# One scan for the first block's chain, and a hand-written order of VectorE and ScalarE for the opening, in a linear-recurrence-and-experts kernel on one core

## Chip, cores, metric

One core of a Trainium2 chip runs the kernel. The metric is the device time of one execution in microseconds; the kernel before took 1793.38 (median of three runs, 1790.74 to 1793.52). TensorE (PE), VectorE (DVE), ScalarE (ACT), GpSimd (POOL) and the queues that issue DMAs (SP's above all) each work through a list of their own in order, and wait for each other by semaphores.

## What is computed

For 4 batches of 768 positions and 8 heads of 48 channels a complex recurrence runs over time, and its result feeds a mixture of 8 experts with Sinkhorn-balanced weights. Cut to what matters:

```python
scale = np.minimum(mag, 0.999) / (mag + 1e-06)      # mag = |a|
for t in range(S):
    S_re, S_im = a * S (complex) + k_t v_t^T         # kv goes into the real part
    y[t] = q_t @ S_re
x = y as [3072, 384]
P = softmax-like, 8 Sinkhorn passes over x @ w_gate
for e in range(8):
    out += P[:, e:e+1] * (np.maximum(x @ w1[e], 0) @ w2[e])
```

Precision is near fp32: a matrix operand is split into a high part and a residue (both fp32r), and each product is three matmuls (`hh*wh`, `hh*wl`, `hl*wh`).

## The kernel before

The 3072 rows are 12 *blocks* of 256 positions, and each block is two *chunks* of 128. Phase 1 goes over the blocks. Per block it has two kinds of work.

The **chain** (`elem`, `chain`, `scan`) normalises the decay `a` and multiplies it up along time within each chunk. `chain` begins with a square on ACT (L390), a sum on DVE (L391), two ACT steps (L392, L393), two DVE steps (L394, L395), an ACT step (L396), two DVE steps (L397, L398) and the product with `z` (L400). Then `scan` calls `cmul` twelve times: each call multiplies complex numbers with two products (L283, or L286 in pieces), a difference (L287) and a sum (L288), all on DVE. A closing part squares the result (ACT, L409), sums (DVE, L410), takes a root and a square (ACT, L413, L414), has three DVE steps (L415 to L417) and makes the decayed keys `kh` (L420) and queries `z` (L422), two halves each. For blocks 1 to 11 the chain runs at once over both chunks (128 x 768 elements per plane); for block 0 `elem` runs it twice, once per chunk, at 128 x 384.

The **mix** copies `kh` and `z` with 24 small DMAs into the per-head layout `ks` and `qs` (L441; six for each of `ks` and `qs` of each chunk, all on SP's queue). Then come, per chunk: transposed keys `ktp` (PE, L460, copied to `kt` by ACT, L462), `scores` (`sp`, PE L474, with a causal mask copied by DVE into `sc`, L477), the state increment `U` (PE, L469), small copies of the chunk's total decay (ACT, L502 to L504), the outputs `y` (PE, L491), the state update (DVE, L517 and L524 to L528, `st`), and the split of `y` into `xh` (ACT, L530) and `xl` (DVE, L531).

The **experts** 0 and 1 follow one block behind: 16 *expert steps* per block, each a layer-1 product `ph` (PE, L179 to L181, reading `xh` and `xl`), relu copies `hh` and `hf` (ACT, L185, L186) and the residue `hl` (DVE, L187); layer 2 (`po`, L158 to L160) runs three steps later. While block i is mixed, PE works on the expert steps of block i-1, and the mix's PE parts are put between them from step `LEAD[i]` on (11 for block 1). Phase 2 does the other six experts with a fast-matrix-multiplication scheme (L798 to L800, L894 to L896).

Ahead of the first expert step is the **opening**. Beside block 0's chain and mix it prepares the sixteen weights of experts 0 and 1. `load_w` handles twelve: DMA into a raw tile `wr` (L123; four raw tiles in turn), a rounded copy on ACT (L124), and for each half j a PE difference `wd` of raw and rounded (L128 by the identity, L129 by its negative) that ACT copies as residue (L130). The last four come as twelve pieces of 256 columns through `load_thirds` (L139, L140, L143 to L145), eight pieces ahead.

In phase 1 the order of PE is the order of the code (`manual_schedule` for PE alone). DVE, ACT and the DMA queues are ordered by the framework's scheduler, with hints: `issue_after` (emit behind another instruction), and `behind`, an ordering edge that puts a mask copy behind a `cmul` of the next block's scan.

Of the kernel before, what the change touches and what calls it, by code (L numbers as in the profile page):

```python
# [1 line left out]

# [12 lines left out]
C = H * D  # L15
# [39 lines left out]
class Net:  # L55
# [9 lines left out]
    def build(self):  # L65
# [3 lines left out]
        with ExitStack() as ctx:  # L69
# [30 lines left out]
            self.fl = cst.tile([128, ns * (NCT * NCH + 2) + 2], F32, name="fl")  # L100
# [18 lines left out]
    def load_w(self, e, f, wx):  # L119
# [3 lines left out]
        self.wl = nc.sync.dma_start(raw, self.w[e, f])  # L123
        nc.scalar.activation(t[:, 0, :], raw, AF.Copy)  # L124
        for j in range(2):
            cs = slice(j * C, j * C + C)
            d = (self.psB if j else self.psA).tile([128, C], F32, tag="po" if j else "ph", name=f"wd{e}_{f}_{j}")
            nc.tensor.matmul(d, self.ident, raw[:, cs], start=True, stop=False)  # L128
            nc.tensor.matmul(d, self.nident, t[:, 0, cs], start=False, stop=True)  # L129
            nc.scalar.activation(t[:, 1, cs], d, AF.Copy)  # L130

    def load_thirds(self, e, f, wx):
        nc = self.nc
        t = self.wt[e, f] = wx.tile([128, 2, 2 * C], F32R, tag="w", name=f"w{e}_{f}")
        for j in range(2 * C // SUB):
            cs = slice(j * SUB, j * SUB + SUB)
            raw = self.hp.tile([128, SUB], F32, tag=("hh", "hl")[(f * 3 + j) % 2], name=f"wr{e}_{f}_{j}")
            with self.tc.issue_after(self.wl.ins):
                nc.sync.dma_start(raw, self.w[e, f, :, cs])  # L139
            nc.scalar.activation(t[:, 0, cs], raw, AF.Copy)  # L140
            yield
# [3 lines left out]
            nc.scalar.activation(t[:, 1, cs], d, AF.Copy)  # L145

# [43 lines left out]
    def phase1(self, c1, ca):  # L190
# [29 lines left out]
        self.xs, self.vt, self.kqd, self.ql, self.masks, self.acts = {}, {}, {}, {}, {}, []  # L220
# [11 lines left out]
        for i in range(ns):  # L232
            mix = self.mix(i)
            if i == 0:
                n = 0
                while True:
                    with tc.issue_after(self.act0.ins), tc.issue_after(self.dve0.ins):
                        if next(mix, self) is self:
                            break
                    with tc.issue_after(self.act0.ins):  # L240
                        for _ in range(2):
                            if late and next(late[0], self) is self:
                                late.pop(0)
                                next(late[0], None) if late else None
                    n += 1
                for g in late:
                    for _ in g:
                        pass
# [5 lines left out]
            lg = self.logits(i - 1)  # L254
            for n in range(2 * NF):
# [7 lines left out]
            if i + 1 < ns:  # L263
                self.elem(i + 1)
# [3 lines left out]
        for f in range(2):  # L268
            self.moe.send((ns - 1, 0, f))
            next(lg)  # L270

    def cmul(self, L, R, n, alloc):
# [6 lines left out]

        a, b = tmp("a"), tmp("b")  # L280
        for o, k in ((a, 0), (b, 1)):
            if len(sh) == 4:
                V.tensor_tensor(o, L, R[:, k:k + 1].broadcast_to(sh), ALU.mult)  # L283
            else:
                for j in range(2):
                    V.tensor_tensor(o[:, j], L[:, j], R[:, k], ALU.mult)  # L286
        V.tensor_tensor(R[:, 0], a[:, 0], b[:, 1], ALU.subtract)  # L287
        self.last = V.tensor_tensor(R[:, 1], a[:, 1], b[:, 0], ALU.add)  # L288
        self.cm.append(self.last)
# [5 lines left out]
    def elem(self, i, scratch=False):  # L295
# [8 lines left out]
        if not scratch:  # L304
            with ExitStack() as st:
                if i > 1:
                    st.enter_context(self.tc.issue_after(self.ql[i - 2].ins))
                nc.sync.dma_start(z, self.aqk[i, :, 0:2])
            with self.tc.issue_after(self.ql[i - 1].ins):
                nc.sync.dma_start(qk, self.aqk[i, :, 2:4])  # L310
            nc.sync.dma_start(vt, self.v[i])

            def alloc(nm):
# [8 lines left out]
            self.chain(i, slice(0, NCH), zt, qk, alloc)  # L322
            return

        def cut(t, n):
            return t.rearrange("p a (c n) t -> p a c n t", n=NCH)[:, :, :, n, :]

        for n in range(NCH):
            for a in range(2):
                (nc.sync if a else nc.scalar).dma_start(cut(z, n)[:, a], cut(self.aqk[i, :, 0:2], n)[:, a])  # L330
        nc.sync.dma_start(qk, self.aqk[i, :, 2:4])
        nc.sync.dma_start(vt, self.v[i])
        kh = tmp.tile([128, 2, G, CH], F32, tag="kh", name="kh0", bufs=1)
        self.kqd[i] = (kh, zt)
        tt = {nm: self.xp.tile([128, G, CH], F32R, tag=tg, name=f"{nm}0").bitcast(F32)
              for nm, tg in (("x", "xh"), ("y0", "xl"), ("zz", "xh"), ("a", "xl"))}
        tt["b"] = tmp.tile([128, G, CH], F32, tag="t1", name="b0", bufs=5)
        tt["g0"] = tt["zz"]

        for n in range(NCH):  # L340
            def alloc(nm, n=n):
# [805 lines left out]
```

## Time and profile before

| | us |
|---|---|
| median of three runs | 1793.38 |
| lowest, highest | 1790.74, 1793.52 |
| the profiled execution | 1792.06 |
| its span (first to last instruction) | 1790.3 |
| PE busy | 1751.3 |
| DVE busy | 1366.8 |
| ACT busy | 733.6 |

The page shows one execution. Busy times are sums over instructions; neighbours on an engine overlap by about 0.1 us, so busy time can exceed the time from start to start. In rows of the timeline the columns are start, length, engine, line, operation, output and inputs, shape and count, and in brackets the idle time ahead of the first instruction and what ended it. In the view of waits each row has the total, how many times, and the longest. In rows of the view of windows, the window, its length, and busy time with instruction counts for PE, PEld, DVE, ACT and POOL, then the granted clock of PE, the mean share of the DMA engines, and GB/s. In the groups by line, the numbers behind the first bar are the busy time and the mean of one in ns.

### The profile page before, as it was taken

What the parts mean: (1) busy time and instruction counts of PE and PEld (TensorE: products, weight loads), DVE (VectorE), ACT (ScalarE), POOL (GpSimd) and SP (SyncE); (2) the same over time, 40 slices, a digit from 0 to 9 for tenths busy, and PEclk for the clock granted to TensorE, in tenths of its full rate; (3) what the DMA queues carried; (4) which work ended last, traced back from release to release, by engine and by line L of the source; (5) the groups of instructions that cost most, each with busy time, mean ns of one, the idle gap of its engine ahead of it and who ended that gap; (6) DMA issues with size and microseconds to landing.
All of it is one profiled execution on the core that took longest, in us unless ns stands there. A gap on an engine that the chain in (4) does not pass through costs nothing.

```text
span 1790.3 us, 30678 instructions
## 1 busy us (share of the span) xinstructions
PE 1751.3 (98%) x12024; PEld 1725.8 (96%) x12024; DVE 1366.8 (76%) x3036; ACT 733.6 (41%) x1609; POOL 6.4 (0%) x15
## 2 busy tenths in 40 slices
PE   5889999999999999999999999999999999999998
PEld 3889999999999999999999999999999999999998
DVE  7898999999983678777777767687767777776754
ACT  7544544555543544443332424243433333332321
POOL 1000000000000000000000000000000000000000
PEclk9899999999999999999999999999999999999999
DMA  6333333334343420111111101232111111010100
GB/s 215 95 119 110 119 119 119 119 114 119 103 105 104 135 89 27 53 53 46 45 54 50 48 18 54 76 111 63 45 52 38 54 54 50 22 54 18 45 27 29
DMA packets 133689, 132.85 MB, mean 74 GB/s; under 512 B 10400, under 2 KB 125856, under 8 KB 133536
## 3 DMA queue, kind: packets, MB, share of 16 engines
q1 hardware_dynamic: 132736, 130.41, 24.3%
q8 instruction: 96, 1.57, 0.4%
q14 instruction: 57, 0.47, 0.1%
q10 hardware_dynamic: 800, 0.39, 0.1%
HBM read 88.22 MB, written 23.59 MB: 62 GB/s over the span
## 4 chain that ended last, share of the span: by engine, by line
PE 91%; DVE 6%; DMA 1%; ACT 1%; issue 1%; SPq 0%; ACTq 0%; DVEq 0%
PE po L800 11%; PE po L799 11%; PE po L798 11%; PE P L894 10%; PE P L896 10%; PE P L895 10%; PE po L158 4%; PE ph L180 4%; PE ph L181 4%; PE ph L179 3%; PE po L159 3%; PE po L160 3%; PE sp L474 2%; PE y L491 2%; PE U L469 1%; DMA wr<-in_w_dram 1%
## 5 line engine op out<-in xcount | busy, mean ns | idle before, releaser
L800 PE MATMUL po<-wc,hl 128*128 128x384 f32 x1152 | 385.0, 334 | 0.0
L799 PE MATMUL po<-wc,hh 128*128 128x384 f32 x1152 | 384.8, 334 | 0.0
L798 PE MATMUL po<-wc,hh 128*128 128x384 f32 x1152 | 384.8, 334 | 0.0
L914 ACT ACTIVATE hh<-c 128x384 fp32r<-128x384 f32 x384 | 201.6, 526 | 347.0 <-DVE c L904 347.0
L919 DVE SCALAR_TENSOR_TENSOR hl<-c,hh 128x384 fp32r<-128x384 f32 x384 | 212.5, 553 | 50.5 <-ACT hh L914 36.3
L909 ACT ACTIVATE s<-P 128x384 f32<-128x384 f32 x192 | 94.1, 490 | 317.8 <-PE P L896 317.8
L800 PEld LDWEIGHTS po<-wc,hl 128*128 128x128 f32 x1152 | 216.3, 188 | 0.3 <-DVE hl L919 0.2
L798 PEld LDWEIGHTS po<-wc,hh 128*128 128x128 f32 x1152 | 216.3, 188 | 0.0
L799 PEld LDWEIGHTS po<-wc,hh 128*128 128x128 f32 x1152 | 216.3, 188 | 0.0
L185 ACT ACTIVATE hh<-ph 128x256 fp32r<-128x256 f32 x192 | 73.5, 383 | 231.1 <-PE ph L181 230.6
L180 PE MATMUL ph<-xl,w 128*128 128x256 f32 x576 | 162.7, 282 | 3.3 <-DVE xl L531 3.3
L181 PE MATMUL ph<-xh,w 128*128 128x256 f32 x576 | 162.4, 282 | 0.0
L179 PE MATMUL ph<-xh,w 128*128 128x256 f32 x576 | 162.0, 281 | 0.0
L894 PE MATMUL P<-B,wa 128*128 128x384 f32 x480 | 160.8, 335 | 0.1
L896 PE MATMUL P<-B,wa 128*128 128x384 f32 x480 | 160.3, 334 | 0.0
L895 PE MATMUL P<-B,wa 128*128 128x384 f32 x480 | 160.3, 334 | 0.0
L158 PE MATMUL po<-w,hh 128*128 128x384 f32 x384 | 136.7, 356 | 0.0
L159 PE MATMUL po<-w,hh 128*128 128x384 f32 x384 | 129.6, 337 | 0.0
L160 PE MATMUL po<-w,hl 128*128 128x384 f32 x384 | 129.4, 337 | 0.0
L904 DVE TENSOR_TENSOR c<-P,u 128x384 f32<-128x384 f32 x192 | 106.7, 556 | 22.0 <-PE P L896 20.4
L187 DVE TENSOR_TENSOR hl<-hf,hh 128x256 fp32r<-128x256 f32 x192 | 81.0, 423 | 48.3 <-ACT hf L186 46.9
L180 PEld LDWEIGHTS ph<-xl,w 128*128 128x128 f32 x576 | 108.8, 189 | 4.0 <-DVE xl L531 4.0
(189 smaller groups left out, 3579.0 us busy)
## 6 DMA issues: line engine op xcount, KB each, us to landing
raw<-in_w_dram SPq DMA_DIRECT2D x96, 384.0 KB, 3.1
qs<-z SPq DMA_DIRECT2D x144, 64.5 KB, 2.6
qk<-in_aqk_dram SPq DMA_DIRECT2D x12, 768.0 KB, 4.7
ks<-kh SPq DMA_DIRECT2D x144, 64.0 KB, 2.6
ye_d<-yst SPq DMA_DIRECT2D x48, 192.0 KB, 1.9
y<-ye_d SPq DMA_DIRECT2D x48, 192.0 KB, 2.4
z<-in_aqk_dram SPq DMA_DIRECT2D x11, 768.0 KB, 6.6
B<-x_d SPq DMA_DIRECT2D x40, 192.0 KB, 3.4
```

What stands on the lines that cost most here:

```text
L158: nc.tensor.matmul(po[k], hh[:, s], w2h, start=f == 0, stop=False)
L179: nc.tensor.matmul(ph, w[:, 0, cs], xh[:, ct, :], start=(ct == 0), stop=False)
L180: nc.tensor.matmul(ph, w[:, 0, cs], xl[:, ct, :], start=False, stop=False)
L181: nc.tensor.matmul(ph, w[:, 1, cs], xh[:, ct, :], start=False, stop=(ct == NCT - 1))
L798: nc.tensor.matmul(po[k], hh[:, s], w2[:, 0, i], start=first, stop=False)
L799: nc.tensor.matmul(po[k], hh[:, s], w2[:, 1, i], start=False, stop=False)
L800: nc.tensor.matmul(po[k], hl[:, s], w2[:, 0, i], start=False, stop=last)
L894: nc.tensor.matmul(ps, t[:, 0, k], x[:, 0], start=first, stop=False)
L895: nc.tensor.matmul(ps, t[:, 0, k], x[:, 1], start=False, stop=False)
L896: nc.tensor.matmul(ps, t[:, 1, k], x[:, 0], start=False, stop=last)
L914: A.activation(hh, c, AF.Relu)
L919: V.scalar_tensor_tensor(hl, c, 0.0, hh.bitcast(F32), ALU.max, ALU.subtract)
```

## The change

1. Block 0's chain runs once over both chunks, as for the other blocks. Its planes come in two DMAs of 128 x 768 elements instead of four of half the size. The two products of L400 become one instruction for all blocks, and the two flags of the split chain go.
2. `chain`, `scan` and `cmul` become generators: they hand control back behind each DVE step with an estimate of its time. `load_w` is cut into a fetch, a copy and two residues, and `load_thirds` fetches eight pieces ahead by itself.
3. `mix` is cut into parts (`chunk`: `keys`, `scores`, `state`, `turn`, `outs`, `update`, `evict`). `mix` for blocks 1 to 11 calls them as before.
4. A new function `opening` writes out what is issued up to the eleventh expert step, and the order of DVE and ACT is manual within it too. There keys come behind scores, and chunk 1's keys and state increment around the first expert step. SP's queue is still ordered by the scheduler.

```diff
     def load_w(self, e, f, wx):
...
         self.wl = nc.sync.dma_start(raw, self.w[e, f])
+        yield
         nc.scalar.activation(t[:, 0, :], raw, AF.Copy)
+        yield
         for j in range(2):
...
             nc.scalar.activation(t[:, 1, cs], d, AF.Copy)
+            yield
...
+        ahead = 2 * (LAG + 1)
+        for q in todo[:ahead]:
+            fetch(*q)
+        yield
+        for n, (f, j) in enumerate(todo):
+            cs = slice(j * SUB, j * SUB + SUB)
+            raw, t = raws[n], self.wt[e, f]
             nc.scalar.activation(t[:, 0, cs], raw, AF.Copy)
...
+            if n + ahead < len(todo):
+                fetch(*todo[n + ahead])
+            yield
...
-        self.elem(0, True)
-        for f in range(NF):
-            self.load_w(0, f, wx)
-        with tc.issue_after(self.acts[0].ins):
-            for f in range(RING - NF):
-                self.load_w(1, f, wx)
-        late = [self.load_thirds(1, f, wx) for f in range(RING - NF, NF)]
...
-                with tc.issue_after(self.gl.ins):
-                    self.elem(1)
-                self.behind(0, 1, 0, k=1)
-                self.behind(0, 1, 1, k=3)
-                continue
...
+        with tc.manual_schedule(engines={mybir.EngineType.DVE, mybir.EngineType.Activation}):
+            self.opening(wx)
...
+    def opening(self, wx):
+        def adv(g, us):
+            while us > 0:
+                d = next(g, None)
+                if d is None:
+                    return
+                us -= d
+
+        def ops(g, k):
+            for _ in range(k):
+                next(g, None)
...
+        g0 = self.elem(0)
+        full = [self.load_w(n // NF, n % NF, wx) for n in range(RING)]
+        for k in range(4):
+            whole(k)
+        g1 = self.elem(1)
+        w = iter([(k, q) for k in range(RING) for q in range(3)])
+
+        def split(k):
+            for _ in range(k):
+                n, q = next(w, (None, None))
+                if n is None:
+                    return
+                next(full[n])
+                if q == 2:
+                    whole(n + 4)
...
+        while not self.scanned:
+            ops(g0, 4)
+            split(2)
+        ops(g1, 2)
+        ops(g0, 1)
+        ops(g1, 2)
+        split(2)
+        ops(g0, 3)
+        split(RING * 3)
+        for _ in g0:
+            pass
+        late = self.load_thirds(1, range(RING - NF, NF), wx)
+        next(late)
+        a, b = self.chunk(0, 0), self.chunk(0, 1)
+        ops(g1, 1)
+        ops(late, 8)
+        adv(g1, 6.5)
+        a.scores(0)
+        a.scores(1)
+        a.keys(0)
+        a.keys(1)
+        adv(g1, 1.0)
+        a.state(0)
+        a.state(1)
+        a.turn()
+        a.outs(0)
+        a.outs(1)
+        ops(late, 2)
+        adv(g1, 1.6)
+        a.evict()
+        a.update()
+        ops(late, 2)
+        adv(g1, 1.6)
+        b.scores(0)
+        adv(g1, 0.3)
+        b.scores(1)
+        adv(g1, 2.2)
+        b.outs(0)
+        b.outs(1)
+        b.evict()
+        b.keys(0)
+        b.keys(1)
+        self.lg = self.logits(0)
+        for n in range(LEAD[1]):
+            self.moe.send((0, n // NF, n % NF))
+            if n in (1, 2):
+                next(self.lg)
+            if n == 0:
+                b.state(0)
+                b.state(1)
+                b.turn()
+            if n == LEAD[1] - 3:
+                b.update()
+            adv(g1, 1.6)
...
-        for a in range(2):
-            V.tensor_tensor(z[:, a], z[:, a], x, ALU.mult)
...
+        V.tensor_tensor(z, z, x.unsqueeze(1).broadcast_to(sh), ALU.mult)
+        yield 2 * one
```

`full` holds the twelve weights, `late` the pieces, `g0` and `g1` the chains of blocks 0 and 1, `a` and `b` block 0's chunks; `whole(k)` starts the fetch of weight k, and `split(k)` issues the next k of copy, residue, residue. Lines of the changed kernel: the copy is L126, the residues L133, the pieces L146, L156 and L160; the squares L484 and L508, the sums L486 and L510, the roots L511 and L512; `ks`/`qs` L545; `xh` L632 and `xl` L633.

How this moves instructions, by the order of each engine. First ACT, before, from the middle of the weights to the closing square of block 0's first chunk (`w0_7` is expert 0's weight 7, `wd0_7_1` its residue's second half, `kh0` the tile that takes block 0's squares).

```order
L124 ACTIVATE w0_7_450<-wr0_7_451 128x768
L130 ACTIVATE w0_5_426<-wd0_5_0_430 128x384
L130 ACTIVATE w0_5_426<-wd0_5_1_434 128x384
L130 ACTIVATE w0_6_438<-wd0_6_0_442 128x384
L130 ACTIVATE w0_6_438<-wd0_6_1_446 128x384
L409 ACTIVATE kh0_208<-z0_199 128x6x128
L130 ACTIVATE w0_7_450<-wd0_7_0_454 128x384
L130 ACTIVATE w0_7_450<-wd0_7_1_458 128x384
```

The same stretch of ACT now, up to the closing square, which is one instruction for both chunks.

```order
L126 ACTIVATE w0_7_309<-wr0_7_310 128x768
L133 ACTIVATE w0_7_309<-wd0_7_0_373 128x384
L133 ACTIVATE w0_7_309<-wd0_7_1_377 128x384
L126 ACTIVATE w1_0_329<-wr1_0_330 128x768
L133 ACTIVATE w1_0_329<-wd1_0_0_389 128x384
L133 ACTIVATE w1_0_329<-wd1_0_1_397 128x384
L126 ACTIVATE w1_1_345<-wr1_1_346 128x768
L133 ACTIVATE w1_1_345<-wd1_1_0_406 128x384
L133 ACTIVATE w1_1_345<-wd1_1_1_410 128x384
L508 ACTIVATE kh0_208<-z0_201 128x1536
```

Before, a copy stood two weights ahead of its residues, and the closing square came behind seven weights' residues. Now each weight is finished before the next is begun, and ten weights stand ahead of the square.

Second, SP's queue before, from the last pieces that go ahead of the copies (`wr1_6_1` is piece 1 of expert 1's weight 6; `ks0` and `qs0` are chunk 0's, `ks1` and `qs1` chunk 1's).

```order
L139 DMA wr1_6_1_666<-in_w_dram 128x256
L441 DMA ks0_177<-kh0_208 16x8x128 x6
L441 DMA qs0_175<-z0_199 16x8x129 x6
L139 DMA wr1_6_2_696<-in_w_dram 128x256
L441 DMA ks1_178<-kh0_208 16x8x128 x6
L441 DMA qs1_176<-z0_199 16x8x129 x6
L139 DMA wr1_7_0_704<-in_w_dram 128x256
L139 DMA wr1_7_1_754<-in_w_dram 128x256
```

SP's queue now.

```order
L146 DMA wr1_6_1_467<-in_w_dram 128x256
L545 DMA ks0_177<-kh0_208 16x8x128 x6
L545 DMA qs0_175<-z0_201 16x8x129 x6
L545 DMA ks1_178<-kh0_208 16x8x128 x6
L545 DMA qs1_176<-z0_201 16x8x129 x6
L146 DMA wr1_6_2_501<-in_w_dram 128x256
L146 DMA wr1_7_0_509<-in_w_dram 128x256
L146 DMA wr1_7_1_516<-in_w_dram 128x256
L146 DMA wr1_7_2_523<-in_w_dram 128x256
```

The piece between the chunks' copies and the ones behind them now all stand behind the 24 copies.

Third, ACT ahead of the first expert step, before: chunk 1's `xh0` (of `y0_1`) and what stands around it.

```order
L145 ACTIVATE w1_6_658<-wd1_6_2_699 128x256
L530 ACTIVATE xh0_510<-y0_1_638 128x3x128
L145 ACTIVATE w1_7_703<-wd1_7_0_750 128x256
L145 ACTIVATE w1_7_703<-wd1_7_1_757 128x256
L145 ACTIVATE w1_7_703<-wd1_7_2_764 128x256
L185 ACTIVATE hh0_0_0_892<-ph0_0_0_882 128x256
```

ACT at this place now (`sq1`, `g01`, `z1` and `x1` belong to block 1's closing part, `sq2` to block 2's first square).

```order
L160 ACTIVATE w1_7_508<-wd1_7_2_685 128x256
L508 ACTIVATE sq1_717<-z1_226 128x1536
L511 ACTIVATE g01_719<-x1_718 128x768
L484 ACTIVATE sq2_1356,fl_91<-z2_1350 128x1536
L512 ACTIVATE g01_719<-g01_719 128x768
L514 ACTIVATE z1_226<-z1_226 128x12
L516 ACTIVATE fl_91<-x1_718 128x6
L632 ACTIVATE xh0_469<-y0_1_726 128x3x128
```

Chunk 1's `xh` now stands behind block 1's closing square, its roots and block 2's first square, which came behind the first expert steps before.

More of the change, by code (lines that the diff above doesn't have):

```diff
@@ new lines, in chunk, with keys @@
+        self.ql[i] = dma
+        R = qs[:, :, CH]
+        first = (i % self.nsub == 0) and c == 0
+        lastc = (i % self.nsub == self.nsub - 1) and c == NCH - 1
+        S0, S1 = self.st[self.ist], self.st[1 - self.ist]
+        if not lastc:
+            self.ist = 1 - self.ist
+        cs = slice(c * CH, c * CH + CH)
+        kts, sss, at = {}, {}, {}
+        def keys(g):
+            if lastc:
+                return
+            if i == 0:
+                kt_p = self.psB.tile([128, 4, SK], F32, tag="po", name=f"ktp{i}_{c}_{g}")
+            else:
+                kt_p = self.psS.tile([128, 4, SK], F32, tag="s", name=f"ktp{i}_{c}_{g}")
+            for j in range(4):
+                nc.tensor.transpose(kt_p[:, j, :], ks[:, 4 * g + j, :], self.ident[:SK, :SK])
+            kts[g] = tmp.tile([128, 4, SK], F32, tag="kt", name=f"kt{i}_{c}_{g}", bufs=2)
+            self.kt = nc.scalar.activation(kts[g], kt_p, AF.Copy)
@@ new lines, in state, with scores @@
+        def state(g):
+            if lastc:
+                return
+            if g == 0:
+                at["U"] = self.psY.tile([SK, H, D], F32, tag="U", name=f"U{i}_{c}")
+            for j in range(4):
+                h = 4 * g + j
+                nc.tensor.matmul(at["U"][:, h, :], kts[g][:, j, :], vt[:, c, slot(h):slot(h) + D], start=True, stop=True)
+        def scores(g):
+            sp = self.psS.tile([128, 4, CH], F32, tag="s", name=f"sp{i}_{c}_{g}")
+            for j in range(4):
+                nc.tensor.matmul(sp[:, j, :], ks[:, 4 * g + j, :], qs[:, 4 * g + j, :CH], start=True, stop=True)
+            ss = sss[g] = self.sc[self.isc]
+            self.isc = 1 - self.isc
+            self.masks[i, c, g] = nc.vector.copy_predicated(ss, self.mask, sp)
@@ L500, in mix, with turn @@
+        def turn():
             if not lastc:
@@ L534, in mix @@
                     nc.sync.dma_start(self.x_d[i // NS][:, i % NS, a], t.bitcast(F32).rearrange("p c (j t) -> p c j t", t=CH))
-            if i == 0 or c == NCH - 1:
+        return SimpleNamespace(keys=keys, state=state, scores=scores, outs=outs, turn=turn, update=update, evict=evict)
+    def mix(self, i):
+        for c in range(NCH):
+            k = self.chunk(i, c)
+            k.keys(0)
+            k.keys(1)
+            yield
+            k.scores(0)
+            k.scores(1)
+            k.state(0)
+            k.state(1)
+            k.turn()
+            yield
+            yield
+            k.outs(0)
+            k.outs(1)
+            k.update()
+            k.evict()
+            if c == NCH - 1:
                 yield
```

349 lines of the change are left out of this document (165 added, 184 removed).

## The prediction

> **What bounds the kernel now.** The page comes first. TensorE (PE) is busy for almost the whole span, so a microsecond counts only where PE stands still or runs slowly.
>
> ```profile
> span 1790.3 us, 30678 instructions
> PE 1751.3 (98%) x12024; PEld 1725.8 (96%) x12024; DVE 1366.8 (76%) x3036; ACT 733.6 (41%) x1609; POOL 6.4 (0%) x15
> ```
>
> The view of waits for PE then tells where it stands still, and the timeline when.
>
> ```profile
> PE ktp L460 <- DMA ks<-kh: 5.9, 2, 3.7
> PE wd L143 <- ACT kt L462: 4.5, 1, 4.5
> PE ktp L460 <- ACT w L145: 4.2, 1, 4.2
> PE ph L180 <- DVE xl L531: 3.3, 3, 2.2
> ...
> PE sp L474 <- DMA qs<-z: 0.5, 1, 0.5
> ```
>
> ```profile
> 71.32 0.28 PE L179 MATMUL ph<-xh,w 128*128 128x256 f32 x1
> ...
> 98.88 1.73 PE L460 MATMUL ktp<-ident,ks 112*128 112x112 f32 x8 [3.70 <-DMA ks<-kh]
> ...
> 125.44 0.39 PE L180 MATMUL ph<-xl,w 128*128 128x256 f32 x1 [2.19 <-DVE xl L531]
> ```
>
> The row at 71.32 is the first matmul of the first expert step ("step 0"). All ahead of it is opening: PE has little to do there, and the end of the program moves with step 0. Behind it 3.7 (ks), 0.5 (qs) and 3.3 (xl) us are waited, 7.5 in all; the row at 125.44 is block 1's first step, 54.1 behind step 0. So the change is worth what it does to two instants: step 0, and block 1's first step.
>
> The windows give the clock.
>
> ```profile
> 28.00:32.00 4.00, 2.12 (x8) 1.32 (x8) 3.93 (x17) 3.72 (x8) 0.00 (x0) 1.00 0.83 262
> 40.00:44.00 4.00, 0.00 (x0) 0.00 (x0) 1.81 (x6) 2.25 (x5) 0.00 (x0) 0.56 0.15 36
> ...
> 60.00:64.00 4.00, 4.00 (x16) 3.64 (x16) 2.78 (x7) 1.78 (x6) 0.00 (x0) 0.50 0.85 243
> ...
> 124.00:128.00 4.00, 2.56 (x12) 2.56 (x13) 3.94 (x9) 2.14 (x3) 0.00 (x0) 0.73 0.62 240
> ```
>
> With PE busy half the time the granted clock stays at 1.00; four idle microseconds take it to 0.56. Some 2.5 us are lost to the low clock around the two long waits (0.27 of 4 us in the last row, as much again around it).
>
> **The change part by part.** Nothing is taken from PE. What moves is the order on VectorE (DVE), ScalarE (ACT) and the DMA queue of SP, ahead of step 0. I follow the new order row by row with the durations of the old trace.
>
> *The weights on ACT.* Before, ACT copied a weight (L124) ahead of the residues (L130) of the one before it. Now each weight is finished before the next copy: copy, PE, residue, PE, residue.
>
> ```profile
> 29.27 2.30 ACT L124 ACTIVATE w<-wr 128x768 fp32r<-128x768 f32 x3
> ...
> 35.05 0.49 ACT L130 ACTIVATE w<-wd 128x384 fp32r<-128x384 f32 x1 [0.33 <-PE wd L129]
> ```
>
> ```profile
> 30.15 0.45 PE L129 MATMUL wd<-w,nident 128*128 128x384 f32 x1 [1.88 <-ACT w L124]
> 30.43 0.81 PE L128 MATMUL wd<-wr,ident 128*128 128x384 f32 x2
> ```
>
> A copy takes 0.84 and PE starts 0.04 behind it (29.27 + 2.30 less two overlaps is 30.11, PE at 30.15). The first residue's matmul needs 0.45; the second half's L128 is issued at 0.32 behind the copy and its L129 is through at 1.31; the residue then holds ACT for 0.40 before the next copy. That is 0.84 + 0.04 + 1.31 + 0.40, less overlap, 2.57 us a weight, where ACT's own work is 1.65. Ten weights stand ahead of the square that ends block 0's scan: 25.7 us. Block 1's first square and root steps stand among them (3.2, of which 1.0 falls into the gaps), and the first weight meets a slow PE (0.8): 28.7.
>
> When does it begin? The chain's steps at the new width are block 1's rows of the old trace:
>
> ```profile
> 49.55 0.83 ACT L393 ACTIVATE zz<-y 128x768 f32<-128x768 f32 x1
> ...
> 52.54 0.94 ACT L396 ACTIVATE zz<-y,bm 128x768 f32<-128x768 f32 x1 [2.08 <-DVE y L395]
> ...
> 69.70 0.49 ACT L530 ACTIVATE xh<-y 128x384 fp32r<-128x384 f32 x1 [1.54 <-PE y L491]
> ...
> 80.97 1.49 ACT L409 ACTIVATE sq<-z 128x1536 f32<-128x1536 f32 x1
> ```
>
> ```profile
> 50.50 0.96 DVE L394 TENSOR_TENSOR x<-x,zz 128x768 f32<-128x768 f32 x1 [0.98 <-ACT zz L393]
> ...
> 70.76 0.55 DVE L531 TENSOR_TENSOR xl<-y,xh 128x384 fp32r<-128x384 f32 x1
> ...
> 92.03 1.82 DVE L420 TENSOR_TENSOR kh<-x,z 128x768 f32<-128x768 f32 x2
> ```
>
> ```profile
> 6.12 0.84 ACT L390 ACTIVATE kh<-z 128x768 f32<-128x768 f32 x1 [0.47 <-DMA z<-in_aqk_dram]
> ...
> 6.96 0.83 ACT L390 ACTIVATE kh<-z 128x768 f32<-128x768 f32 x1
> ```
>
> The two planes land as the four halves did, by 6.7 (between 6.1 and 7.0, these rows). From there: square 1.6 with its sum, DVE 1.0, two root steps of 0.83 with a sum 1.9, two on DVE 2.0, ACT 0.9: 14.1. ACT reaches the closing square at 14.1 + 28.7 = 42.8.
>
> *The scan.* DVE goes on with 1.0 and 1.8 to 16.9, then the scan at full width.
>
> ```profile
> L283 DVE TENSOR_TENSOR cm_a<-z 128x384 f32<-128x384 f32 (+5 forms) x10 | 4.1, 407 | 0.2
> ...
> L287 DVE TENSOR_TENSOR z<-cm_a,cm_b 128x192 f32<-128x192 f32 (+7 forms) x12 | 3.6, 304 | 0.2
> ...
> L286 DVE TENSOR_TENSOR cm_a<-z 128x126 f32<-128x126 f32 (+1 forms) x4 | 1.6, 415 | 0.0
> ```
>
> cm_b of L283 has nearly as much as cm_a, L288 as L287, and the other L286 as this one: 18.5 busy, 17 with neighbours overlapping, and one step of block 1 (0.95): it ends at 34.8. One scan for two saves DVE work, but DVE then stands 8.0 us for ACT.
>
> *To the keys.* Behind the square: x 1.0, two roots 1.7, two on DVE 2.0, block 1's two (1.9), block 1's ACT step with the multiply that stands ahead of the keys (2.3), half of kh 0.9; with the square's 1.5 that is 11.3. The first plane of kh is there at 54.1.
>
> *The queue.* Both chunks' 24 copies now go one after the other, and the last four weight pieces stand behind them.
>
> ```profile
> 36.58 3.76 SPq L441 DMA_DIRECT2D qs<-z  x6
> ...
> 46.88 3.88 SPq L441 DMA_DIRECT2D ks<-kh  x6
> ...
> 55.12 0.99 SPq L139 DMA_DIRECT2D wr<-in_w_dram  x2
> ```
>
> ```profile
> 49.22 0.42 ACT L140 ACTIVATE w<-wr 128x256 fp32r<-128x256 f32 x1 [0.49 <-DMA wr<-in_w_dram]
> ...
> 57.47 0.42 ACT L140 ACTIVATE w<-wr 128x256 fp32r<-128x256 f32 x1 [3.45 <-DMA wr<-in_w_dram]
> ```
>
> Six copies take about 3.9, so 24 take 15.7: the queue is free at 69.8. Before, chunk 0's twelve were out by 40.3, because its half of the scan was finished first. A piece lands 2.35 behind its issue (55.12 to 57.47) or more; I take 3.1: 72.9. The same wait is in the old trace (3.45), fifteen us earlier.
>
> *To step 0.* Three more prices of DVE:
>
> ```profile
> 48.18 1.34 DVE L477 COPY_PREDICATED sc<-mask,sp 128x512 f32<-128x512 uint8 x2
> ...
> 52.96 0.55 DVE L524 TENSOR_TENSOR sa<-U,rr 112x384 f32<-112x384 f32 x1
> ...
> 73.67 0.42 DVE L187 TENSOR_TENSOR hl<-hf,hh 128x256 fp32r<-128x256 f32 x1
> ```
>
> ACT's hand order puts two pieces ahead of chunk 0's xh: 0.42, some 0.4 on PE, and about 0.42 for the residue, 1.17 each with overlap, then xh 0.49: counted from the landing, +2.9. DVE is in strict order: xl 0.55 and four of state update, 0.55 and a small gap each (+5.7), four multiplies of the scan (+7.5), two masks (1.3) and two adds (0.9) (+9.7), the last product (+11.3). Only then can ACT square block 1 (1.5), DVE step (1.0), and ACT take root 0.85, block 2's square 1.5, root 0.8 and two small ones 0.25; all of these stand ahead of chunk 1's xh in ACT's queue: +17.2. xh 0.49 and xl 0.55: +18.2. Step 0 at 91.1, against 71.3: **19.8 late**.
>
> *Behind step 0.* One part moved to behind it:
>
> ```profile
> 48.14 1.68 PE L469 MATMUL U<-v,kt 128*112 128x48 f32 x16
> ```
>
> Block 1's chain is nearly done by then, so its ks copies leave about 7 us behind step 0 and are landed long before PE asks: the waits of 3.7 and 0.5 go, with the slow clock behind them. What is late next is block 1's xl again. DVE reaches block 2's scan about 19.5 behind step 0 (an estimate: its last seven steps on block 1 and seven first ones on block 2, 13 us, stand between the hl, which PE hands out one by one); then scan 17, two updates 5.6, masks 2.5, seven hl of 0.34 behind their overlap, an xl, 47.4; the square, one step and xl on top: 51.0. PE's own work until there is some 47 (54.1 less waits of 3.7, 0.5 and 2.2 and the slow clock, and 1.5 more for chunk 1's U, 1.68 less overlap), so it waits about 4. 51.0 against 54.1 gives 3.1 back. From there both orders are alike; I give 0.4 more for the merged multiply and an earlier state update.
>
> The rest (two flag checks fewer, a dropped ordering edge) lies under PE's work: nothing, or some 0.3 us if it is not covered.
>
> Sum: the profiled execution took 1792.06 (span 1790.3 and 1.76 around it). 1792.06 + 19.8 - 3.5 = **1808.4**. The median of the runs shown is 1793.38, 1.3 above it; I make no difference of that.
>
> **A rule against the rows.** The weight preparation now leaves PE gaps of about 0.4 us in each 1.3. The row at 28 to 32 (2.12 busy of 4, clock 1.00) says that such gaps leave the clock up, and the sum uses full speed from 20 us on.
> The Trainium skill, "TensorE: Matmul & The Clock Gate", section "A second HAM failure mode: psum-queue depth-cycling", tells of a kernel whose short idles between groups made the clock fall and rise again. By that rule the rival below would be the forecast; this trace's row speaks against it, but it shows only one such stretch.
>
> **The rivals.** *The clock stays low in the weights* (0.10). At the low clock two L128 take longer:
>
> ```profile
> 13.32 1.48 PE L128 MATMUL wd<-wr,ident 128*128 128x384 f32 x2
> ```
>
> 1.48 against 0.81, and L129 0.17 more: 0.84 a weight, 8 us for ten, 0.8 of it in the sum: 1815.6.
>
> *ACT is not the limit* (0.10). If the weights keep ahead of the scan, the 8.0 us on the square fall away: 1800.4. The serial order speaks against it.
>
> *Faster* (0.07). Block 1's chain being ready removes the waits behind step 0, 7.5, with 2.5 of slow clock. That pays if step 0 is no later than 71.3 + 10 - 1.5 for the moved U, about 80. Were ACT no limit, the last pieces would land at 64.9. In the old trace step 0 came 13.8 behind that landing (57.5 to 71.3), and PE ran at half speed for some 5 us of it (0.50 in the row at 60); at full speed that is 11.3, step 0 at 76.2, and the time 1792.1 + 4.9 + 1.5 - 10 = 1788.5. Against it: the eight DVE and ACT steps that the new order puts between landing and step 0.
>
> *No change* (0.03): the same with 13.8, step 0 at 78.7, 1791.
>
> Mine has 0.70; its own range is 1803 to 1814 (0.8 on landings, 2 on the weights, 2 to 3 on each of the last two parts). With the neighbours 1799 to 1817. 0.2% (3.6 us) is about what a measurement of this kernel can tell from no change: faster 0.07, same 0.03, slower 0.90.
>
> **What would show it.** Right: copies and residues strictly in turn at about 2.6 us a weight; DVE idle about 8 us ahead of the closing step of block 0's scan; the queue's 24 copies from about 54 to 70; ACT waiting for a weight piece at about 73; the first ph at 88 to 94; no wait for ks at block 1. Wrong: the first ph before 80, a closing square right behind the scan, or waits behind step 0 as large as before.

## The result, and the profile after

The changed kernel takes 1815.03 us (median of four runs, 1813.68 to 1815.93), the kernel before, run beside it on the same chip, 1792.06 (1789.60 to 1793.52): a ratio of 1.0129, with a 95% interval of 1.0111 to 1.0147. It is slower by 23 us. The forecast was 1808.4, with a range of its own of 1803 to 1814, and of 1799 to 1817 with the neighbouring cases: the direction came true, and the time lies just above the forecast's own range.

The page of the changed kernel: PE has 15 us more busy time for the same 12024 matmuls, and the span has 22.9 more.

```profile
span 1813.2 us, 30580 instructions
PE 1766.4 (97%) x12024; PEld 1730.3 (95%) x12024; DVE 1363.0 (75%) x2953; ACT 734.6 (41%) x1598; POOL 6.4 (0%) x15
```

The view of waits for PE (total, times, longest). The wait for `ks` has gone from behind the first expert step; new are the ten waits for weight copies, the longest (5.0 us) right behind block 0's closing square, and the 6.0 us for `xh`.

```profile
PE wd L132 <- ACT w L126: 14.4, 10, 5.0
PE wd L131 <- DMA wr<-in_w_dram: 11.7, 1, 11.7
PE ph L197 <- ACT xh L632: 6.8, 2, 6.0
PE wd L158 <- DMA wr<-in_w_dram: 2.1, 1, 2.1
PE ph L198 <- DVE xl L633: 2.1, 2, 1.4
```

ACT in the timeline: the last two of the ten weights ahead of block 0's closing square, then the wait for a weight piece, chunk 0's `xh`, and the steps of block 1 and block 2 that stand ahead of chunk 1's `xh`.

```profile
38.24 0.83 ACT L126 ACTIVATE w<-wr 128x768 fp32r<-128x768 f32 x1
...
40.82 0.83 ACT L126 ACTIVATE w<-wr 128x768 fp32r<-128x768 f32 x1
...
43.39 1.47 ACT L508 ACTIVATE kh<-z 128x1536 f32<-128x1536 f32 x1
...
73.95 0.42 ACT L156 ACTIVATE w<-wr 128x256 fp32r<-128x256 f32 x1 [3.85 <-DMA wr<-in_w_dram]
...
77.14 0.49 ACT L632 ACTIVATE xh<-y 128x384 fp32r<-128x384 f32 x1
...
86.14 1.48 ACT L508 ACTIVATE sq<-z 128x1536 f32<-128x1536 f32 x1 [5.79 <-DVE z L394]
88.65 0.84 ACT L511 ACTIVATE g<-x 128x768 f32<-128x768 f32 x1 [1.02 <-DVE x L510]
89.39 1.47 ACT L484 ACTIVATE sq<-z 128x1536 f32<-128x1536 f32 x1
...
91.81 0.46 ACT L632 ACTIVATE xh<-y 128x384 fp32r<-128x384 f32 x1
```

DVE at the same places. The bracket is what it stood ahead of the row: 10.50 us at the closing square, and another 14.3 at the two `xl` and the first two `hl` shown (`hl` is L205 here).

```profile
44.89 0.96 DVE L510 SCALAR_TENSOR_TENSOR x<-kh 128x768 f32<-128x768 f32 x1 [10.50 <-ACT kh L508]
...
77.66 0.56 DVE L633 TENSOR_TENSOR xl<-y,xh 128x384 fp32r<-128x384 f32 x1 [5.07 <-ACT xh L632]
...
92.30 0.56 DVE L633 TENSOR_TENSOR xl<-y,xh 128x384 fp32r<-128x384 f32 x1 [3.69 <-ACT xh L632]
95.72 0.43 DVE L205 TENSOR_TENSOR hl<-hf,hh 128x256 fp32r<-128x256 f32 x1 [2.86 <-ACT hf L204]
100.66 0.42 DVE L205 TENSOR_TENSOR hl<-hf,hh 128x256 fp32r<-128x256 f32 x1 [2.65 <-ACT hf L204]
```

SP's queue: 24 copies one behind the other from 55.0 to 71.3, and the four last weight pieces behind them.

```profile
55.00 3.91 SPq L545 DMA_DIRECT2D ks<-kh  x6
...
66.67 4.66 SPq L545 DMA_DIRECT2D qs<-z  x6
71.45 2.33 SPq L146 DMA_DIRECT2D wr<-in_w_dram  x4
```

PE: the first expert step at 92.32 (71.32 before), the first logits of block 0 at 99.73 (73.49), and block 1's first `xl` at 146.49 (125.44).

```profile
92.32 0.58 PE L197 MATMUL ph<-xh,w 128*128 128x256 f32 x1 [6.02 <-ACT xh L632]
...
94.79 3.08 PE L575 MATMUL U<-v,kt 128*112 128x48 f32 x16
...
99.73 0.41 PE L665 MATMUL lp<-xh,wgs 128*16 128x256 f32 x1
...
146.49 0.39 PE L198 MATMUL ph<-xl,w 128*128 128x256 f32 x1 [1.37 <-DVE xl L633]
```

The windows around the first expert step: PE stands, and then runs eight microseconds at half clock (the granted clock is the third number from the end).

```profile
88.00:92.00 4.00, 0.00 (x0) 0.00 (x0) 0.61 (x1) 3.35 (x7) 0.00 (x0) 0.81 0.00 0
92.00:96.00 4.00, 3.67 (x17) 3.37 (x17) 0.84 (x2) 2.10 (x7) 0.00 (x0) 0.50 0.51 197
96.00:100.00 4.00, 4.00 (x22) 3.86 (x22) 1.97 (x3) 0.25 (x3) 0.00 (x0) 0.50 0.27 93
```

So the 22.9 us of span are: 21.0 at the first expert step, 5.1 more up to block 0's logits, 5.0 given back between these and the last block's logits (516.98 us, 521.94 before), and 1.7 in phase 2. (Here and below, where no row is shown, logits are dated by the start of their first weight load, 99.52 for block 0.) The giving back isn't steady: block 1's logits come 19.5 late, block 2's 20.2, the last block's 21.2. The 1.7 of phase 2 is no effect that I can pin on the change: there the matmuls of the changed kernel run a little slower throughout (1154 in 200 us, 1156 before), and those of the kernel with one scan alone do the same.

### The profile page after: what moved, and what is told of

Its sections match the earlier page's. It is cut to its first block, busy times and chain, and to the rows that moved or that the text cites. A ratio compares the mean times of both kernels' runs of the same rounds, so it can differ in the third digit from the quotient of the medians.

```text
span 1813.2 us, 30580 instructions
## 1 busy us (share of the span) xinstructions
PE 1766.4 (97%) x12024; PEld 1730.3 (95%) x12024; DVE 1363.0 (75%) x2953; ACT 734.6 (41%) x1598; POOL 6.4 (0%) x15
## 4 chain that ended last, share of the span: by engine, by line
PE 90%; DVE 6%; ACT 2%; issue 1%; SPq 1%; DMA 0%; ACTq 0%; DVEq 0%
PE po L921 11%; PE po L920 11%; PE po L922 11%; PE P L1016 10%; PE P L1018 10%; PE P L1017 10%; PE po L176 4%; PE ph L198 4%; PE ph L199 4%; PE ph L197 4%; PE po L177 3%; PE po L178 3%; PE sp L580 2%; PE y L600 2%; PE U L575 1%
## 5 line engine op out<-in xcount | busy, mean ns | idle before, releaser
L1031 ACT ACTIVATE s<-P 128x384 f32<-128x384 f32 x192 | 94.1, 490 | 319.1 <-PE P L1018 319.0
L205 DVE TENSOR_TENSOR hl<-hf,hh 128x256 fp32r<-128x256 f32 x192 | 80.7, 423 | 53.5 <-ACT hf L204 49.4
L197 PEld LDWEIGHTS ph<-xh,w 128*128 128x128 f32 x576 | 109.1, 189 | 7.8 <-ACT xh L632 7.7
```

The source lines that it names most:

```text
L197: nc.tensor.matmul(ph, w[:, 0, cs], xh[:, ct, :], start=(ct == 0), stop=False)
```

## The experiments

All start from the changed kernel unless the text says otherwise. The theory: three delays add up, **A** the serial order of copy and residues on ACT, **B** the 24 copies ahead of the last pieces, **C** the steps of block 1 and 2 ahead of chunk 1's `xh`; and **D** the low clock behind the wait. The rival is that merging the scan costs by itself. Ratios are to the kernel before, run beside each.

**A alone undone.**

```diff
-        w = iter([(k, q) for k in range(RING) for q in range(3)])
+        w = iter([(0, 0)] + [x for k in range(RING) for x in
+                 ([(k + 1, 0)] if k + 1 < RING else []) + [(k, 1), (k, 2)]])
```

> The changed kernel, but the copy of each weight now stands ahead of the residues of the weight before it, as in the kernel before the change. Theory A (the serial order of copy and residues on ACT delays the closing square of block 0): ten weights take about 18 us in place of 28, the 10.5 us for which DVE waits for the closing square shrink to 1 to 3, and everything behind it moves as a whole: first expert step at about 84 (92.3 in the changed kernel), time about 1807. Rival (the serial order is hidden, because the queue of SP or the chain of block 1 decides): the closing square moves, the first expert step stays within 2 us of 92.3, time 1813 to 1816. Rival (merging the scan is what costs): no more than 2 us are won, since DVE's own work is untouched.

1805.70 us, ratio 1.0083 (1.0067 to 1.0100); first expert step at 81.54. In ACT's timeline the copies behind the fourth come 1.48 to 1.63 us apart in place of 2.57, and the square waits for DVE, not DVE for the weights.

```profile
28.39 0.90 ACT L126 ACTIVATE w<-wr 128x768 fp32r<-128x768 f32 x1
...
29.87 0.92 ACT L126 ACTIVATE w<-wr 128x768 fp32r<-128x768 f32 x1
...
34.66 1.48 ACT L508 ACTIVATE kh<-z 128x1536 f32<-128x1536 f32 x1 [0.35 <-DVE z L394]
```

The square is 8.7 earlier and the kernel 9.3 faster: A is shown, with its size, and neither rival.

**B alone undone.**

```diff
-        a, b = self.chunk(0, 0), self.chunk(0, 1)
+        a = self.chunk(0, 0)
         ops(g1, 1)
         ops(late, 8)
+        b = self.chunk(0, 1)
```

> The changed kernel, but the 12 small copies of chunk 1 are written behind the last weight pieces, so that SP's queue has the four pieces between the two chunks' copies. Theory B (the 24 copies hold back the pieces, and the pieces hold back xh of chunk 0): the pieces land some 5 to 7 us earlier (about 67 in place of 73.95), chunk 1's copies end 2 us later and are not waited for, first expert step 3 to 6 us earlier (86 to 89), time 1809 to 1812. Rival (DVE's strict order is late by itself): the pieces land earlier and the first expert step stays within 1 us, time 1814 to 1816.

1811.58 us, ratio 1.0111 (1.0095 to 1.0128); first expert step at 89.48. The time is the expected one, 3.5 faster; the step is 2.8 earlier, a little less than the 3 to 6 given. The pieces are issued from 63.65 on, not 71.45:

```profile
63.65 1.95 SPq L146 DMA_DIRECT2D wr<-in_w_dram  x4
```

**C alone undone,** first by moving the steps behind chunk 1's `xh` and `xl`.

```diff
-        adv(g1, 2.2)
         b.outs(0)
         b.outs(1)
         b.evict()
+        adv(g1, 2.2)
```

> The changed kernel, but chunk 1's outputs and its xh and xl stand ahead of block 1's closing square, roots and block 2's first square. Theory C (those ACT and DVE steps are what PE waits for last, the single wait of 6.0 us ahead of the first expert step): first expert step about 5 us earlier (87 to 88), DVE stands about 2 us for xh, time 1809 to 1811. Rival (chunk 1's outputs are late by their scores and masks): under 1 us won. Rival (the shift is paid back at block 1, whose chain is 2 us later): first expert step 5 us earlier, time only 2 to 3 us better.

1815.62 us, ratio 1.0139 (1.0122 to 1.0156): no gain at all. That is the time of the rival that chunk 1's outputs are late by themselves, but not for its reason, for the first expert step did come earlier, at 85.12. The wait had only moved: PE's next work is chunk 1's `U`, whose `kt` now stood behind the same ACT steps (view of waits):

```profile
PE U L575 <- ACT kt L566: 7.3, 2, 7.0
```

So the two copies of the keys were put ahead too.

```diff
-        adv(g1, 2.2)
         b.outs(0)
...
         b.keys(1)
+        adv(g1, 2.2)
```

> The changed kernel, but chunk 1's outputs, xh, xl and the two copies of its keys (kt) stand ahead of block 1's closing square, roots and block 2's first square. Theory C (PE stands 6.0 us for what is behind these ACT steps, and runs at half clock for some 8 us behind it): first expert step at about 85 (92.3), no wait of U for kt, clock back at 1.00 within 4 us, time 1804 to 1808. Rival (the closing part of block 1 is then late by as much, and it is paid at block 1's first expert step as a longer wait for xl): first expert step at 85, xl waited for 5 to 9 us longer, time 1811 to 1815.

1812.90 us, ratio 1.0116 (1.0099 to 1.0133); first expert step at 86.83, last block's logits at 616.37 (616.50 in the changed kernel). The time is the rival's, its mechanism is not (the longest wait for `xl` is 1.2): now the first step's relu copies stand behind block 1's square on ACT, and PE waits for them two steps later.

```profile
PE ph L197 <- ACT hf L204: 3.8, 1, 3.8
```

**Everything together.** The diffs of A, B and C's first form in one kernel:

> The edits of the first three experiments together: the copy a weight ahead of the residues, the four pieces ahead of chunk 1's copies, and chunk 1's xh ahead of block 1's closing square. If the times add (1805.7 for the first, 3.2 won by the second, nothing by the third, whose wait of 7.0 us only went over to kt behind the first expert step): 1801 to 1804, with a wait of about 7 us of chunk 1's U for kt right behind the first expert step. Rival (with two delays gone the third edit is worth something): under 1799.

1807.06 us, ratio 1.0084 (1.0067 to 1.0101), with the expected 7.0 us of `U` on `kt`, and 4.8 slower than the sum. And with C's second form:

> The changed kernel with the copies of weights a weight ahead of the residues, the four pieces ahead of chunk 1's copies, and chunk 1's outputs, xh and key copies ahead of block 1's closing square: the three delays that I hold responsible, all taken away. If they are the whole loss: first expert step at 70 to 74, time 1788 to 1795. Rival (DVE's strict order behind the keys is what is left): first expert step at 75 to 80, time 1796 to 1800. Rival (block 1's xl is late instead): first expert step early, a wait of over 6 us for xl at block 1, time 1795 to 1799.

1805.81 us, ratio 1.0074 (1.0057 to 1.0091). The first expert step came at 79.61 (12.7 earlier than in the changed kernel), 9.2 us of it reached the end; all three forecasts were lower (1788 to 1800). With A undone alone the time was 1805.70, so B and C together bring nothing once A is undone. My theory of three delays that add had fallen.

**DVE and ACT left to the scheduler,** PE's order and the one scan kept.

```diff
-        with tc.manual_schedule(engines={mybir.EngineType.DVE, mybir.EngineType.Activation}):
-            self.opening(wx)
+        self.opening(wx)
```

> The changed kernel with DVE and ACT left to the scheduler; PE's order and the one scan stay as changed. The scheduler puts about half of block 1's scan between block 0's scan and its closing part, and all sixteen weights but the last pieces ahead of the closing square on ACT. My theory (what counts is the place of the closing square, whoever sets it): square at 45 to 50, first expert step 90 to 97, block 1's chain early, time 1810 to 1820. Rival (the hand order of DVE and ACT is the cost, by its strictness): time 1792 to 1798, like the kernel before with one scan alone.

1800.35 us, ratio 1.0049 (1.0033 to 1.0066): neither forecast. The closing square stands where it stands in the changed kernel, and PE even waits 20.1 us for `ks`; yet the first expert step comes at 80.66.

```profile
43.19 1.49 ACT L507 ACTIVATE kh<-z 128x1536 f32<-128x1536 f32 x1
```

```profile
PE sp L579 <- DMA ks<-kh: 20.1, 1, 20.1
```

By the time of the square ACT has copied all sixteen weights and has all but four pieces' residues, and DVE, which stands 10.5 us there in the changed kernel, is well into block 1's scan: it waits nowhere 0.8 us or more between 12 and 62 us. That led to another count: how long DVE does nothing.

**Block 1's chain not advanced** between chunk 0's outputs and the first expert step.

```diff
         ops(late, 2)
-        adv(g1, 1.6)
         a.evict()
         a.update()
         ops(late, 2)
-        adv(g1, 1.6)
         b.scores(0)
-        adv(g1, 0.3)
         b.scores(1)
-        adv(g1, 2.2)
         b.outs(0)
```

> The changed kernel, but between chunk 0's outputs and the first expert step DVE and ACT advance block 1's chain no more (the four steps of together 5.7 us are left out there; the chain goes on behind the first expert step, 1.6 us a step as before). Theory C' (what ACT and DVE do for block 1 in strict order costs PE wherever PE stands right behind it; it costs little where PE has layer-2 work to do meanwhile): first expert step at 83 to 86, no wait of over 2 us behind it, time 1804 to 1809. Rival (the work is only put off, and block 1's first expert step comes as late as in the changed kernel): first expert step at 83 to 86, block 1's first logits within 2 us of 149.6, time 1812 to 1816.

1819.94 us, ratio 1.0147 (1.0130 to 1.0164): slower than either theory gave and than the changed kernel, though the first expert step is 6.6 earlier. DVE had nothing to do ahead of chunk 0's `xl`:

```profile
79.38 0.56 DVE L629 TENSOR_TENSOR xl<-y,xh 128x384 fp32r<-128x384 f32 x1 [7.46 <-ACT xh L628]
```

With the edits of A and B as well:

> The same, with the copies of weights a weight ahead of the residues and the four pieces ahead of chunk 1's copies. If the three delays add (9.4 and 3.5 measured, some 8 for this one): first expert step at 70 to 74, block 1's first logits at 128 to 131, time 1791 to 1796, no slower than the kernel before. Rival (DVE's and ACT's work up to block 1's xl is the bound once the first expert step is early): first expert step at 70 to 74, block 1's first logits at 135 or later, a wait of over 5 us behind the first expert step, time 1798 to 1803.

1810.50 us, ratio 1.0098 (1.0081 to 1.0115): the first expert step at 73.52, almost as early as before the change, and still 18 us lost, more than either theory gave. Block 1's logits, at 133.2, lie between what the two theories gave (3.2 later than before); and the blocks behind it come later still, by 9.5 us at block 2 and 15.6 at block 5.

**One scan alone,** put into the kernel before the change.

```diff
-        for n in range(NCH):
-            for a in range(2):
-                (nc.sync if a else nc.scalar).dma_start(cut(z, n)[:, a], cut(self.aqk[i, :, 0:2], n)[:, a])
+        for a in range(2):
+            (nc.sync if a else nc.scalar).dma_start(z[:, a], self.aqk[i, :, a])
...
-            self.chain(i, slice(n, n + 1), zt, qk, alloc)
+        self.chain(i, slice(0, NCH), zt, qk, alloc)
```

> The kernel before the change with one part of the change alone: block 0's chain runs once over both chunks; DVE and ACT stay with the scheduler, and keys stay ahead of scores. My theory (hand order A and C cost most, the merged scan only what it does to the queue: the 24 copies come in one go at the end, ahead of the last four pieces): closing square at about 35, copies about 45 to 61, first expert step 76 to 79, time 1796 to 1801. Rival (the merged scan itself costs all): first expert step 90 or later, time 1812 to 1816. Rival (the merged scan saves DVE work and pays): time under 1790.

1794.76 us, ratio 1.0021 (1.0011 to 1.0031); first expert step at 75.42. By the medians the merged scan costs 2.4 us, by the ratio 2.0 to 5.6, of the 23: it is not what costs all, as long as the scheduler orders DVE and ACT. Whether it costs more under the hand order no run shows, since none has that order with the scan split.

Taken together the runs split the loss, roughly, since they were not all run side by side: one scan 2.4, the rest of the change with DVE and ACT left to the scheduler some 6 (8.6 for that kernel, less 2.4), and the hand order of DVE and ACT 14.7 (1815.03 less 1800.35). A is 9.3 of the last.

**Extra matmuls to keep PE busy** in the 6.0 us wait.

```diff
         b.evict()
+        d = self.psA.tile([128, SUB], F32, tag="ph", name="warm")
+        for _ in range(36):
+            self.nc.tensor.matmul(d[:, :128], self.ident, self.ident, start=True, stop=True)
```

> The changed kernel with 36 extra matmuls of the identity by itself (128 x 128, some 5 us at the full clock, result unused) in PE's order ahead of chunk 1's key transposes, in the stretch in which PE otherwise stands 6.0 us for xh. Theory D (the stretch behind the first expert step is slow because the granted clock fell to 0.50 while PE stood; the first logits come 7.2 us behind the first expert step in place of 2.1): first expert step within 1 us of 92.3, clock 1.00 behind it, first logits 2 to 4 us earlier than 99.5, time 1811 to 1813. Rival (the 7.2 us are chunk 1's U and waits, not the clock): first logits within 1 us of 99.5, time 1814 to 1816. Rival (the clock falls all the same): rows of ph at 0.21 us apart as before.

1813.85 us, ratio 1.0125 (1.0109 to 1.0142), between the two forecasts, and not to be told from the changed kernel. The extra matmuls took 8.3 us, so the first expert step came 1.8 late, at 94.12. The clock stayed up, and block 0's logits were 1.7 earlier all the same. But at block 1's `xl` PE waits 1.36 us, the clock falls there, and the gain is gone at block 1's logits (149.49; 149.52 in the changed kernel). The windows, two rows of PE, and the first product of block 2's scan on DVE here and in the changed kernel:

```profile
92.00:96.00 4.00, 4.00 (x40) 4.00 (x39) 0.56 (x1) 1.73 (x5) 0.00 (x0) 1.00 0.52 193
...
144.00:148.00 4.00, 3.11 (x13) 3.11 (x14) 2.46 (x5) 3.60 (x8) 0.00 (x0) 0.63 0.59 232
```

```profile
85.28 8.31 PE L354 MATMUL warm<-ident 128*128 128x128 f32 x72
...
144.89 0.48 PE L198 MATMUL ph<-xl,w 128*128 128x256 f32 x1 [1.36 <-DVE xl L636]
```

```profile
115.20 0.55 DVE L389 TENSOR_TENSOR cm_a<-z 128x384 f32<-128x384 f32 x1
```

```profile
117.19 0.55 DVE L386 TENSOR_TENSOR cm_a<-z 128x384 f32<-128x384 f32 x1
```

The same with the edits of A and B:

> The same extra matmuls, with the copies of weights a weight ahead of the residues and the four pieces ahead of chunk 1's copies; block 1's chain stays ahead as in the changed kernel. If the three costs add (9.4, 3.5 and some 3): first expert step at 77 to 80, time 1798 to 1801. Rival (what is repaired is partly the same time): 1802 to 1806.

1805.62 us, ratio 1.0071 (1.0052 to 1.0091; runs from 1801 to 1809): the rival's time; the first expert step, at 87.30, is later than the 77 to 80 expected. With A undone, B and the extra matmuls together bring nothing that these runs can tell.

**A count over all kernels.** The windows give DVE's busy time from 8 us to block 2's first logits; the rest of the window it stood. Before and after:

```profile
8.00:176.90 168.90, 144.91 (x1188) 130.02 (x1189) 147.86 (x403) 91.83 (x220) 0.00 (x0) 0.94 0.43 132
```

```profile
8.00:197.00 189.00, 156.66 (x1187) 131.35 (x1188) 146.89 (x337) 94.13 (x216) 0.00 (x0) 0.90 0.39 118
```

168.90 less 147.86 is 21.0, 189.00 less 146.89 is 42.1. The same for the others, with the start of the first weight load of the last block's logits. All dates are of the profiled executions, some of which are slower than their kernel's median (by 3.4 us in the last kernel with extra matmuls).

| kernel | first expert step | DVE stood | more than before | last block's logits | later than before |
|---|---|---|---|---|---|
| before | 71.3 | 21.0 | | 595.3 | |
| changed | 92.3 | 42.1 | 21.1 | 616.5 | 21.2 |
| A undone | 81.5 | 31.5 | 10.5 | 606.1 | 10.8 |
| B undone | 89.5 | 39.8 | 18.8 | 614.1 | 18.8 |
| C undone, first form | 85.1 | 41.3 | 20.3 | 615.7 | 20.4 |
| C undone, second form | 86.8 | 40.7 | 19.6 | 616.4 | 21.1 |
| A, B, C first form | 75.4 | 33.9 | 12.9 | 608.6 | 13.3 |
| A, B, C second form | 79.6 | 33.6 | 12.6 | 609.8 | 14.4 |
| block 1 not ahead | 85.7 | 48.3 | 27.3 | 622.8 | 27.4 |
| the same, A and B undone | 73.5 | 36.1 | 15.0 | 611.9 | 16.6 |
| extra matmuls | 94.1 | 42.0 | 21.0 | 616.4 | 21.1 |
| extra matmuls, A and B undone | 87.3 | 33.8 | 12.7 | 610.5 | 15.2 |
| one scan alone | 75.4 | 28.8 | 7.8 | 598.8 | 3.5 |
| scheduler's order | 80.7 | 19.5 | -1.5 | 602.2 | 6.9 |

In the eleven kernels with the hand order the time that DVE stands in the opening and the first two blocks gives the lateness at the end within 2.5 us; the first expert step does not (73.5 with 16.6 late, 92.3 with 21.2). The last two rows, with the scheduler's order, do not follow it.

The count is less than it looks, though, since its window ends at block 2's logits. In nine of the eleven kernels DVE has worked 146.9 to 148.7 us in the window (147.9 before), so its standing is, within 1 us, the lateness of block 2's logits, and that date serves better: the end comes 1.0 to 1.1 later than it says, once 1.9. It also fits the last two rows (block 2's logits 2.4 and 6.4 late, the end 3.5 and 6.9). Count and date part only in the two kernels with block 1 not ahead. There DVE had worked 142.6 and 142.4 us and so had 5 us still to do; block 2's logits were 22.0 and 9.5 late, the end 27.4 and 16.6, which is nearer to the count. In the second of them PE waits for `ks` (2.4 us) and twice for ACT's relu copies (0.9 and 0.8) behind block 2's logits.

So what the runs show is that the first expert step alone doesn't decide the end: with block 1 not ahead it is 6.6 earlier, DVE stands 6.2 more, and the kernel is 4.9 us slower. That DVE's standing is the cause is argued from this and not shown, for no run changed it alone. No kernel here beats the one before.

## Why the prediction was right, and where it was off

Step by step, predicted and measured:

- *Front of the chain*: the first square at 6.7, ACT's first copy at 14.1; 6.73 and 14.06.
- *Weights on ACT*: 2.57 us each, the square at 42.8; 2.57 from copy to copy (40.82 to the square at 43.39). The experiment on A confirms the cause.
- *DVE stands for the square*: 8.0 between the scan's end at 34.8 and ACT reaching the square; the scan ended at 34.39, so 9.0, and 10.50 with the square itself.
- *Keys and queue*: `kh` at 54.1, the queue free at 69.8, a piece at 72.9. DVE began `kh` at 53.99 and had its first plane, by its 0.95 us, at 54.9; the queue was free at 71.3 and the piece there at 73.95. One group of copies took 4.66 in place of 3.9, and the piece landed 2.5 behind its issue, where the prediction took 3.1.

```profile
53.99 1.82 DVE L526 TENSOR_TENSOR kh<-x,z 128x768 f32<-128x768 f32 x2
```

- *From the landing to the first expert step*: +18.2; 92.32 less 73.95 is 18.4. In between: chunk 0's `xh` done at +3.7 (2.9), block 1's scan at +12.2 (11.3), chunk 1's `xh` begun at +17.9 (17.2). That the totals agree so well is partly luck: the prediction adds 0.55 for `xl`, which the first matmul does not wait for (its row names `xh`).

The sum for the first expert step was 91.1 against 92.32: the mechanism and its size hold. Of the parts that were undone alone the serial order is the largest: 9.3 of 23.

**The mis-sized term** is "behind step 0", 3.5 us back. Block 1's first `xl` matmul comes 54.17 behind the first expert step, 54.12 before, where the prediction had 51.0: nothing had come back by then. The waits for `ks` and `qs` did go. But DVE reached block 2's scan 24.9 behind the first expert step (117.19), not 19.5, and PE, which was to be through its own work at some 47 and then wait about 4, waited 1.4 there and 0.4 before, so that its work took 52.4.

The step that failed is the clock. PE ran its first two steps and the moved `U` (3.08 us for what took 1.68) at half clock behind its 6.0 us of waiting; eight microseconds at 0.50 cost about 4 (an estimate from the two windows). The prediction quoted windows in which idle microseconds take the clock to 0.56, let that cost go with the `ks` wait, and did not charge it to the new wait that its own +17.2 made. The kernel with extra matmuls supports this: with the clock at 1.00, DVE reached block 2's scan 21.1 behind its first expert step (115.20 less 94.12), and the `xl` matmul came 50.8 behind (144.89), the 51.0 of the prediction.

Yet the clock doesn't account for the whole term. From the `xl` matmul to block 1's logits the changed kernel took 3.0 us, the kernel before 4.6, for the clock didn't fall there this time: 1.5 had come back at block 1's logits. Then 0.7 was lost up to block 2's logits and 1.0 behind them, where the view of waits shows PE waiting for nothing. The prediction put all of this at nothing ("From there both orders are alike"). And the kernel with extra matmuls ends as late as the changed one. Why the gain is lost again stays open.

At the last block's logits the lag is 21.2, so this term is 3.7 off. A further 1.2 is the later first step, and 1.7 phase 2's slower matmuls: together the 6.6 by which the profiled execution (1815.05) missed 1808.4.

*The rivals.* "The clock stays low in the weights" gave 1815.6, nearest of all to the measured time, but that is chance. It came out only in part: the windows of the changed kernel show 0.70 and 0.87 between 24 and 32, 1.00 from 32 to 44.

```profile
24.00:28.00 4.00, 2.67 (x6) 1.59 (x6) 3.73 (x18) 2.33 (x7) 0.00 (x0) 0.70 0.22 85
28.00:32.00 4.00, 3.30 (x10) 1.63 (x9) 3.90 (x15) 2.48 (x5) 0.00 (x0) 0.87 0.53 180
```

In the first form of C, with the same order up to there, these windows show 1.00 and the square stands at 42.52: the dip is worth about 0.9 us, not 8. The rule cited from the Trainium skill, "TensorE: Matmul & The Clock Gate", section "A second HAM failure mode: psum-queue depth-cycling" (short idles between groups make the clock fall and rise again), so agrees with some executions of this stretch and not with others. "ACT is not the limit" falls with the square, which follows the tenth weight without a gap while DVE stands, and with the experiment on A. "Faster" and "no change" needed a first expert step by 80; both fall with 92.3, and the kernel with a step at 73.5 shows that an early step would not have been enough.

**What stays open.** Why the scheduler's order loses 8.6 us with DVE standing no longer than before: the 20.1 us of PE for `ks` lie there, but no run took them apart. What the 5.4 us of the hand order are that A doesn't explain (14.7 less 9.3). And C itself has no price: wherever those ACT steps were put, PE or DVE waited for something else.

## What to carry to other kernels

When an engine's order is written by hand, look for a pair that hands work back and forth (copy, matmul, residue) and leave one item of distance, or the round trip becomes the engine's rate: 2.57 us an item here against about 1.5. An early first step of the busiest engine is worth little if it was bought by putting off work of the engine that feeds it: here a step 6.6 us earlier went with a kernel 4.9 us slower. Follow the feeder to a later date (here block 2's logits), and count what it still has to do then, before arguing from the first step. When a change makes a new wait, charge it for the low clock behind it too. And moving a wait is only a gain if what stands behind the moved work on the strict engine isn't wanted next: here the same ACT steps held up `xh`, then `kt`, then the relu copies.

## What the runs showed of the hardware

- Clock after idle: 6.0 us of waiting left PE at 0.50 for some 8 us. Kept busy over the same stretch with useless matmuls, it stayed at 1.00.
- Two waits of one length went with different clocks: 1.37 us at block 1's `xl` left the clock at 1.00 in the changed kernel, with 1.36 us it fell to 0.63 over 4 us in the kernel with extra matmuls. The stretches ahead are not quite alike: there PE also stood 0.77 and 0.42 us for masks in the 6 us before, in the changed kernel 0.4 in all.

```profile
144.00:148.00 4.00, 2.59 (x16) 2.07 (x16) 2.85 (x5) 2.69 (x5) 0.00 (x0) 1.00 0.81 301
```

- A matmul of 128 x 128 in fp32 is recorded as two, and 36 of them took 8.31 us, 0.23 each; I had reckoned with 0.14.
